# Ten equal token blocks of 464 and 456 columns in place of nine of 512

## The chip, the cores and the metric

The kernel runs on one core of one Trainium2 chip. The metric is the device time of one execution in microseconds. TensorE multiplies, VectorE and ScalarE do the elementwise work, the DMA engines move data between the chip's memory and the core's buffers; SP and ScalarE issue the DMAs.

## What is computed

An attention over packed tokens, then two feed-forward blocks; only the last one is touched by the change. 4608 tokens, all in float32:

```python
x = sm_attn(q, p_packed, p_packed)            # 4608 x 512, p_packed = sm_attn(p, k, v)
a = x @ w1; b = x @ w2                         # 512 -> 1024
x = (a * b @ w3) @ w_out                       # 1024 -> 512
h = x @ w_in                                   # 512 -> 2048
g = np.where(h >= 1, h, np.where(h <= -1, 0.0, (h + 1) ** 2 / 4))
out = g @ w_out2                               # 2048 -> 512
```

## The kernel before

Everything is kept transposed: features on the 128 partitions, tokens along the columns. A product in float32 accuracy is made of three passes over a high and a low part (`PASSES`), so each 128x128 block of weights meets each block of tokens in three matmuls.

The two last products, `x @ w_in` and `g @ w_out2`, are each done as a 2x2 block product with seven block products in place of eight (names A11, S1, S2, A12, S4, S3, A22). One of the two halvings is over the tokens, so tokens go in pairs of blocks. `PAIRS` (line 31) has the first token and the width N of each pair: four pairs of 2 x 512 columns and a short one of 2 x 256.

The first product is the loop over `steps` (line 1057): 8 steps per pair, 40 in all. A step multiplies the seven block products for one block of 128 of the hidden features, six matmuls of N columns each (line 863, 42 per step). ScalarE copies the results of A11, S1 and S2 out of PSUM (`copy`, line 936), VectorE adds the copies to A12, S4 and S3 (`add`, line 940), and ScalarE and VectorE apply the piecewise square (`upper`, `lower_begin`, `lower_relu`, `lower_middle`: lines 871, 874, 877) and the subtractions that the second product's block form needs (`upper_end`, line 904; `lower_end`, line 929). A22 of a step comes one step later, behind S2 of the next step; for the last step it follows at once (line 1112). Results go to the chip's memory, `gd`, from SP's queue (line 888). Two weight tiles per step, `ws`, are loaded in each step.

While a pair is multiplied, the operands of the next pair are made from `x2f` (`x2_tasks`: eleven tasks, seven of them a ScalarE copy, line 730, and a VectorE subtraction, line 731, four a VectorE subtraction alone, line 715). `MID`, `LAST` and `LAST_SHORT` say after which products of which step how many tasks are issued. In the short pair `lower_end` stands ahead of the second addition, the `x2s` tiles hold two operands each, and two steps share an `L` tile.

In the last pair `first_sides` loads what the second product needs first. The second product is the loop over `seq` (line 1160): per pair seven products of four tiles, each tile 12 matmuls of N columns (line 1169). Each tile's operand is loaded from `gd` (`g_load`, line 1007, at most six tiles ahead), for A22 first combined of two loads (line 1016), and split into a high and a low part by ScalarE (line 1024) and VectorE (line 1025). During the first pair five more weight operands are loaded (`w2_load`, line 974) and partly split (lines 982, 983). Results leave by `evacuate` (copies at line 1142, additions at line 1146) and ScalarE's queue (line 1152).

There is no scheduler: each engine works through its instructions in the order in which they are written.

Of the kernel before, what the change touches and what calls it, by code (L numbers as in the profile page):

```python
# [9 lines left out]
F32R = mybir.dt.float32r  # L10
# [12 lines left out]
P = 128  # L23
# [4 lines left out]
CHS = [min(CH, S - i * CH) for i in range(NCH)]  # L28
XD = NT

PAIRS = [(0, 512), (1024, 512), (2048, 512), (3072, 512), (4096, 256)]

A11, S1, S2, A12, S4, S3, A22 = range(7)
STREAM = (S4, A22)
# [25 lines left out]
def fused_kernel(ctx: ExitStack, tc, qT, kT, vv, pb, w1, w2, w3T, wo, win, wout, out):  # L60
# [9 lines left out]
    w2d = [dram.tile([P, 8, 256] if i in PLAIN else [P, 8, 2, 256], F32, name=f"w2{i}") for i in range(7)]  # L70
    gd = [dram.tile([P, 6, 8, n], F32, name=f"g{i}") for i, (_, n) in enumerate(PAIRS)]

# [304 lines left out]
    late = {}  # L377
# [132 lines left out]
    kept = []  # L510
# [189 lines left out]
    x2_t = {}  # L700

    def x2_load(t):
        t0, N = PAIRS[t]
        f = late["f"].tile([P, 4, 1024], F32, name="f", tag="f", bufs=1)
        nc.sync.dma_start(out=f[:, :, :2 * N], in_=x2d[0][:, :, t0:t0 + 2 * N])
        for r in range(2):
            for c in range(2):
                x2f[10 * r + c + 11] = f[:, 2 * r:2 * r + 2, c * N:(c + 1) * N]

    def x2_tasks(t):  # L710

        N = PAIRS[t][1]

        def combine(dst, a, b):
            return lambda: nc.vector.tensor_tensor(out=x2f[dst], in0=x2f[a], in1=x2f[b], op=ALU.subtract)

        room = []

        def parts(q, src):
            def f():  # L720
                if not room:
                    x = late["b1"].tile([P, 2, 2, 512], F32R, name="x2s", tag="x2s", bufs=9)
                    if N == 512:
                        room.append(x)
                    else:
                        x = x.rearrange("p a b (c n) -> p (a b c n)", n=N).rearrange(
                            "p (o a b n) -> p o a b n", o=2, a=2, b=2)
                        room.extend([x[:, 0], x[:, 1]])
                x = x2_t[t, q] = room.pop(0)
                nc.scalar.activation(out=x[:, 0, :, :N], in_=x2f[src], func=AF.Copy)  # L730
                nc.vector.tensor_tensor(
                    out=x[:, 1, :, :N], in0=x2f[src], in1=x[:, 0, :, :N].bitcast(F32), op=ALU.subtract)
            return f
        return [
            parts(A11, 11), combine(11, 12, 11), combine(12, 22, 12), parts(S1, 11), combine(11, 22, 11),
            parts(S2, 11), parts(A12, 21), parts(S4, 22), parts(S3, 12), combine(11, 21, 11), parts(A22, 11),
        ]

    for b in range(1, B):
# [4 lines left out]
        else:  # L744
            spread = {}
            late["f"] = tc.alloc_tile_pool(name="fp", bufs=1, side="left", reuse_waits="tile")
            b1 = late["b1"] = tc.alloc_tile_pool(name="b1", bufs=1, side="left", reuse_waits="tile")
# [43 lines left out]
    def buf(tag):  # L791
        if tag in first:
            return first.pop(tag)
        shape, bufs = KINDS[tag]
        return hp.tile(shape, F32, name=tag, tag=tag, bufs=bufs)
# [9 lines left out]
    def ws_tile(x):  # L805
        return wp.tile([P, 2, 2, P], F32R, name=f"ws{x}", tag=f"ws{x}", bufs=2)

    def ws_load(s, x, eng):
        if s < 8 * len(PAIRS):
            t = ws_t[s, x] = first.pop(f"ws{x}", None) or ws_tile(x)  # L810
            eng.dma_start(out=t.bitcast(F32), in_=wst[s % 8 // 4][:, s % 4, x])
# [37 lines left out]
    def product(s, q):  # L849
        t, i = divmod(s, 8)  # L850
        N = PAIRS[t][1]
        b = BANK[q]
        if q in (A11, S1, A12):
            bank[s, b] = psb(b)
        n, c0 = divmod(i, 4)
        j = 0
        for k in range(2):
            for v, m in PASSES:
                if q in STREAM:
                    w = ws_t[s, STREAM.index(q)][:, k, v, :]  # L860
                else:
                    w = wi_t[q, n][:, k, v, c0 * P:(c0 + 1) * P]
                nc.tensor.matmul(  # L863
                    bank[s, b][:, :N], w, x2_t[t, q][:, m, k, :N],
                    start=(j == 0 and q in (A11, S1, A12)), stop=(j == 5), skip_group_check=True,
                )
                j += 1
# [11 lines left out]
    kept = {}  # L879
# [6 lines left out]
    def store(s, a, n, x):  # L886
        t, i = divmod(s, 8)
        stores.append(lambda: nc.sync.dma_start(out=gd[t][:, a:a + n, i], in_=x))

    def upper(s):  # L890

        N = PAIRS[s // 8][1]
        h = kept[s, 0]
        r = buf("r")[:, :, :N]
        relu(r, h[:, :2, :N])
        square(r)
        for c in range(2):
            smaller(h[:, c, :N], h[:, c, :N], r[:, c])
        store(s, G11, 1, h[:, 0:1, :N])

    def upper_end(s):
        N = PAIRS[s // 8][1]
        h = kept[s, 0]
        nc.vector.tensor_tensor(out=h[:, 2, :N], in0=h[:, 1, :N], in1=h[:, 0, :N], op=ALU.subtract)
        store(s, GT1, 1, h[:, 2:3, :N])

    def lower_begin(s):
        N = PAIRS[s // 8][1]
        r = kept[s, "r"] = buf("r")[:, :, :N]
        relu(r[:, 1], kept[s, 1][:, 1, :N])  # L910

    def lower_relu(s):
        N = PAIRS[s // 8][1]
        relu(kept[s, "r"][:, 0], bank[s, "x"][:, :N])

    def lower_middle(s):

        N = PAIRS[s // 8][1]
        h, r, ps = kept[s, 1], kept[s, "r"], bank.pop((s, "x"))[:, :N]
        square(r)  # L920
        smaller(h[:, 0, :N], ps, r[:, 0])
        smaller(h[:, 1, :N], h[:, 1, :N], r[:, 1])
        store(s, G21, 2, h[:, :2, :N])
        flush_stores()

    def lower_end(s):
        N = PAIRS[s // 8][1]
        h = kept.pop((s, 1))
        nc.vector.tensor_tensor(
            out=h[:, 2:4, :N], in0=h[:, 1:2, :N].to_broadcast([P, 2, N]), in1=kept.pop((s, 0))[:, 1:3, :N],  # L930
            op=ALU.subtract)
        store(s, GT3, 2, h[:, 2:4, :N])

    def copy(tag, ps, N):
        c = buf(tag)[:, :N]
        nc.scalar.activation(out=c, in_=ps[:, :N], func=AF.Copy)  # L936
        return c

    def add(out, ps, c, N):
        nc.vector.tensor_tensor(out=out, in0=ps[:, :N], in1=c, op=ALU.add)  # L940
# [4 lines left out]
    def tasks(n):  # L945
        for _ in range(n):
            if todo:
                todo.pop(0)()
# [80 lines left out]

    MID = {7: 1, 0: 1}  # L1030
    LAST = {2: 2, 3: 1, 4: 1, 5: 1, 7: 2, 0: 1}
    LAST_SHORT = {2: 2, 3: 2, 4: 1, 5: 1, 6: 1, 7: 2, 0: 1}


    def first_sides(s):
# [21 lines left out]
    for s in range(steps):  # L1057
        t, i = divmod(s, 8)
        N = PAIRS[t][1]
        if i == 1 and t + 1 < len(PAIRS):  # L1060
            if t:
                x2_load(t + 1)
            todo = x2_tasks(t + 1)
        if i == 0:
            tasks(1)
        product(s, A11)
        m1 = copy("m1", bank[s, "x"], N)
        if s:
            upper(s - 1)
            if i:  # L1070
                upper_end(s - 1)
            lower_begin(s - 1)
        product(s, S1)
        m5 = copy("m5", bank[s, "z"], N)
        product(s, S2)
        u2 = copy("u2", bank[s, "x"], N)
        if s:
            product(s - 1, A22)
            lower_relu(s - 1)
            lower_middle(s - 1)  # L1080
        product(s, A12)
        kept[s, 0] = buf("U")
        add(kept[s, 0][:, 0, :N], bank.pop((s, "y")), m1, N)
        short = t + 1 == len(PAIRS) and i
        if short:
            lower_end(s - 1)
        to_short = t + (i > 0) + 1 == len(PAIRS)
        tasks(0 if to_short else MID.get(i, 0))
        if t + 1 < len(PAIRS):
            kept[s, 1] = buf("L")  # L1090
        else:
            if s % 2 == 0:
                both = buf("L")
            kept[s, 1] = both[:, :, s % 2 * N:(s % 2 + 1) * N]
        product(s, S4)
        ws_load(s + 2, 0, nc.scalar)
        add(kept[s, 0][:, 1, :N], bank.pop((s, "z")), u2, N)
        product(s, S3)
        add(kept[s, 1][:, 1, :N], bank[s, "x"], m5, N)
        if i == 7 and not short:  # L1100
            lower_end(s - 1)
        tasks((LAST_SHORT if to_short else LAST).get(i, 0))
        if s and i < 7 and not short:
            if i == 0:
                upper_end(s - 1)
            lower_end(s - 1)
        ws_load(s + 1, 1, nc.sync)
        flush_stores()
        for w in {0: (A11, S1), 1: (S2, A12, S3)}.get(s, ()):
            wi_load(w, 1)  # L1110
        first_sides(s)
# [48 lines left out]
    for x, (t, q, j) in enumerate(seq):  # L1160
        N = PAIRS[t][1]
        b = BANK[q]
# [82 lines left out]
```

## Time and profile before

| | us |
|---|---|
| median of 3 runs (1269.65 to 1274.02) | 1270.3 |
| the profiled execution | 1274.56 |
| its span | 1272.8 |
| TensorE busy with matmuls | 1253.5 |
| VectorE busy | 842.1 |
| ScalarE busy | 695.0 |
| first of the two last products begins | 558.4 |
| second of them begins | 918.9 |

Busy time of a matmul contains its drain, which overlaps with the next one; so the distance between the starts of two groups tells what a matmul costs in a row, and idle time in front of a group is shown with the instruction that ended it.

### The profile page before, as it was taken

To read this page: it belongs to the slowest core of one execution; us is meant where nothing else is said; L and a number is where in the kernel's file an instruction comes from. 1 tells how busy PE (TensorE), PEld (TensorE's weight loads), DVE (VectorE), ACT (ScalarE), POOL (GpSimd) and SP (SyncE) were. 2 spreads that over 40 slices of the span, in tenths; PEclk is the share of its full clock that TensorE was granted. 3 is DMA by queue.
4 is the path that set the end of the run, shared out by engine and by line. 5 is a ranking of instruction groups with operands and counts; after the bars stand their busy time and mean duration, and the time that the engine had idled before them with its cause. 6 is when DMAs were issued, how large, how long until landed. Compare 5 with 4: busy or idle time off the path is not lost.

```text
span 1272.8 us, 21501 instructions
## 1 busy us (share of the span) xinstructions
PE 1253.5 (98%) x8344; PEld 1058.3 (83%) x8344; DVE 842.1 (66%) x1356; ACT 695.0 (55%) x1184; POOL 0.7 (0%) x6
## 2 busy tenths in 40 slices
PE   8999999999999999999999999999999999999998
PEld 4468899999989999988888888888888788888888
DVE  3675787857777766707788877878757546464555
ACT  5774546454645553516676767766755443425343
POOL 0000000000000000000000000000000000000000
PEclk9999999999999999999999999999999999999999
DMA  8872566645656533278676586767999868577675
GB/s 317 312 272 84 180 217 209 231 141 212 210 191 232 178 126 135 100 283 310 226 254 247 198 298 221 245 226 255 354 380 330 316 205 293 195 254 272 215 231 183
DMA packets 125302, 297.11 MB, mean 233 GB/s; under 512 B 11024, under 2 KB 47888, under 8 KB 120720
## 3 DMA queue, kind: packets, MB, share of 16 engines
q1 hardware_dynamic: 91888, 241.73, 54.4%
q10 hardware_dynamic: 33312, 54.01, 12.3%
q8 instruction: 65, 1.06, 0.3%
q14 instruction: 37, 0.30, 0.1%
HBM read 195.04 MB, written 100.66 MB: 232 GB/s over the span
## 4 chain that ended last, share of the span: by engine, by line
PE 83%; DMA 7%; ACT 6%; DVE 3%; issue 1%; SPq 0%; ACTq 0%; DVEq 0%
PE psk L417 16%; PE x L1169 15%; PE psk L393 14%; PE x L863 12%; PE z L1169 7%; PE z L863 6%; PE y L1169 4%; PE y L863 3%; PE psk L186 3%; PE psk L521 2%; ACT r L871 1%; DMA raw<-w3T 1%; PE psm L186 1%; ACT x2s L730 1%; ACT r L874 1%
## 5 line engine op out<-in xcount | busy, mean ns | idle before, releaser
L393 PE MATMUL psk<-at,m 128*128 128x288 f32 x1536 | 218.6, 298 | 0.3 <-DVE tb L405 0.3
L393 PEld LDWEIGHTS psk<-at,m 128*128 128x128 f32 x1536 | 205.9, 188 | 13.4 <-issue 7.0
L417 PEld LDWEIGHTS psk<-g,w 128*128 128x128 f32 x1536 | 204.8, 188 | 12.9 <-ACT m L107 8.4
L417 PE MATMUL psk<-g,w 128*128 128x288 f32 x1536 | 210.3, 296 | 0.0
L863 PE MATMUL x<-x2s,wi 128*128 128x512 f32 (+1 forms) x720 | 163.3, 371 | 1.4 <-ACT m L936 1.0
L863 PEld LDWEIGHTS x<-x2s,wi 128*128 128x128 f32 x720 | 126.1, 188 | 27.2 <-ACT m L936 3.7
L1025 DVE TENSOR_TENSOR op<-raw,op 128x1024 fp32r<-128x1024 f32 (+1 forms) x94 | 101.7, 1113 | 70.3 <-ACT op L1024 70.2
L1024 ACT ACTIVATE op<-raw 128x1024 fp32r<-128x1024 f32 (+1 forms) x94 | 87.3, 965 | 70.8 <-DVE raw L1016 31.9
L1169 PE MATMUL x<-op,w 128*128 128x512 f32 (+1 forms) x480 | 102.2, 372 | 2.0 <-DVE op L1025 1.7
L1169 PE MATMUL x<-op,hwi 128*128 128x512 f32 (+1 forms) x480 | 100.4, 368 | 0.0
L1169 PEld LDWEIGHTS x<-op,w 128*128 128x128 f32 x480 | 84.8, 191 | 18.6 <-DVE op L1025 2.6
L1169 PEld LDWEIGHTS x<-op,hwi 128*128 128x128 f32 x480 | 83.1, 188 | 15.8
L405 DVE TENSOR_TENSOR tb<-psk,ta 128x288 f32<-128x288 f32 x128 | 57.9, 454 | 49.8 <-ACT ta L403 29.7
L874 ACT ACTIVATE r<-r 128x1024 f32<-128x1024 f32 (+1 forms) x80 | 78.0, 975 | 2.5
L1025 DVE TENSOR_TENSOR op<-r,op 128x1024 fp32r<-128x1024 f32 (+1 forms) x46 | 50.2, 1117 | 39.1 <-ACT op L1024 39.1
L877 DVE SCALAR_TENSOR_TENSOR U<-U,r 128x512 f32<-128x512 f32 (+1 forms) x80 | 47.5, 635 | 38.4 <-ACT r L874 38.4
L403 ACT ACTIVATE ta<-psk 128x288 f32<-128x288 f32 x128 | 51.5, 404 | 30.5 <-PE psk L393 27.9
L936 ACT ACTIVATE m<-x 128x512 f32<-128x512 f32 (+1 forms) x40 | 22.1, 553 | 84.1 <-PE x L863 66.7
L1024 ACT ACTIVATE op<-r 128x1024 fp32r<-128x1024 f32 (+1 forms) x46 | 43.2, 969 | 41.0 <-DVE r L1016 16.1
L128 ACT ACTIVATE cvt<-raw 128x512 f32<-128x512 f32 (+1 forms) x74 | 49.0, 662 | 28.7 <-DMA raw<-w3T 9.4
L108 DVE TENSOR_TENSOR m<-psk,m 128x512 fp32r<-128x512 f32 x62 | 38.7, 684 | 39.1 <-ACT m L107 39.1
L107 ACT ACTIVATE g<-tb 128x288 fp32r<-128x288 f32 x128 | 56.3, 440 | 11.6 <-DVE tb L405 11.5
(115 smaller groups left out, 1851.7 us busy)
## 6 DMA issues: line engine op xcount, KB each, us to landing
raw<-g SPq DMA_DIRECT2D x86, 512.0 KB, 5.1
g<-L SPq DMA_DIRECT2D x64, 512.0 KB, 3.8
r<-g SPq DMA_DIRECT2D x42, 512.0 KB, 5.3
g<-U SPq DMA_DIRECT2D x64, 256.0 KB, 2.1
ws<-ws SPq DMA_DIRECT2D x42, 256.0 KB, 4.2
v<-vv SPq DMA_DIRECT2D x8, 1280.0 KB, 8.3
wi<-hl ACTq DMA_DIRECT2D x20, 512.0 KB, 3.6
wi<-wi SPq DMA_DIRECT2D x10, 1024.0 KB, 7.7
```

The costliest lines, as they stand in the source:

```text
L107: nc.scalar.activation(out=dst[:, 0], in_=src, func=AF.Copy)
L128: nc.scalar.activation(out=t, in_=words.bitcast(F32)[:, :, 1], func=AF.Prelu, scale=2.0 ** -112, alpha=2.0 ** 32)
L186: nc.tensor.matmul(ps[r][NP * q:NP * q + NP], stat[64 * r:64 * r + 64, NP * q:NP * q + NP], mov(q)[64 * r:64 * r + 64], start=True, stop=True,
L393: nc.tensor.matmul(ps[w][:, :HS], m_tile[b, w, n][:, s, G, c0 * P:(c0 + 1) * P], at_tile[b][:, G, v, hf * HS:(hf + 1) * HS], start=(k == 0 ...
L403: nc.scalar.activation(out=bs, in_=ps[1][:, :HS], func=AF.Copy)
L405: nc.vector.tensor_tensor(out=g, in0=ps[0][:, :HS], in1=bs, op=ALU.mult)
L417: nc.tensor.matmul(ps, w34[kt][:, s, mt * P:(mt + 1) * P], g_t[kt, hf][:, v, :], start=(kt == kts[0] and n == 0), stop=(kt == kts[-1] and ...
L863: nc.tensor.matmul(bank[s, b][:, :N], w, x2_t[t, q][:, m, k, :N], start=(j == 0 and q in (A11, S1, A12)), stop=(j == 5), skip_group_check= ...
L874: nc.scalar.activation(out=r, in_=r, func=AF.Square)
L1024: nc.scalar.activation(out=o[:, :, 0, :N], in_=a[0], func=AF.Copy)
L1025: nc.vector.tensor_tensor(out=o[:, :, 1, :N], in0=a[0], in1=o[:, :, 0, :N].bitcast(F32), op=ALU.subtract)
L1169: nc.tensor.matmul(bank[b][d][:, :N], w2_t[q][j // 2][:, 2 * (j % 2) + k, s, d * P:(d + 1) * P], op[x][:, k, v, :N], start=start and k == ...
```

## The change

`PAIRS` holds five pairs now, three of 2 x 464 and two of 2 x 456 columns; all that treated the short pair in its own way is gone. Every step has one order, that of the long pairs. The matmuls are as many as before. In the tiles, which keep their size, 464 or 456 of 512 columns are used; so a load of two rows of `gd` into one tile is no longer one run of 4096 bytes per partition, but two of 1856 or 1824.

```diff
-PAIRS = [(0, 512), (1024, 512), (2048, 512), (3072, 512), (4096, 256)]
+PAIRS = [(0, 464), (928, 464), (1856, 464), (2784, 456), (3696, 456)]
...
-        room = []
-
         def parts(q, src):
             def f():
-                if not room:
-                    x = late["b1"].tile([P, 2, 2, 512], F32R, name="x2s", tag="x2s", bufs=9)
-                    if N == 512:
-                        room.append(x)
-                    else:
-                        x = x.rearrange("p a b (c n) -> p (a b c n)", n=N).rearrange(
-                            "p (o a b n) -> p o a b n", o=2, a=2, b=2)
-                        room.extend([x[:, 0], x[:, 1]])
-                x = x2_t[t, q] = room.pop(0)
+                x = x2_t[t, q] = late["b1"].tile([P, 2, 2, 512], F32R, name="x2s", tag="x2s", bufs=9)
...
-    LAST_SHORT = {2: 2, 3: 2, 4: 1, 5: 1, 6: 1, 7: 2, 0: 1}
...
-        short = t + 1 == len(PAIRS) and i
-        if short:
-            lower_end(s - 1)
-        to_short = t + (i > 0) + 1 == len(PAIRS)
-        tasks(0 if to_short else MID.get(i, 0))
-        if t + 1 < len(PAIRS):
-            kept[s, 1] = buf("L")
-        else:
-            if s % 2 == 0:
-                both = buf("L")
-            kept[s, 1] = both[:, :, s % 2 * N:(s % 2 + 1) * N]
+        tasks(MID.get(i, 0))
+        kept[s, 1] = buf("L")
         product(s, S4)
...
-        if i == 7 and not short:
+        if i == 7:
             lower_end(s - 1)
-        tasks((LAST_SHORT if to_short else LAST).get(i, 0))
-        if s and i < 7 and not short:
+        tasks(LAST.get(i, 0))
+        if s and i < 7:
```

On VectorE, one step of the last pair stood so before (L929 is `lower_end`, L940 an addition, `m` and `u` the copies, L877 the piecewise square of the next round):

```order
L940 TENSOR_TENSOR U<-y,m_9868 128x256
L929 TENSOR_TENSOR L<-L,U 128x2x256
L940 TENSOR_TENSOR U<-z,u_9893 128x256
L940 TENSOR_TENSOR L<-x,m_9885 128x256
L877 SCALAR_TENSOR_TENSOR U<-U,r 128x256 x2
```

and now (the same lines are L930, L919 and L867):

```order
L930 TENSOR_TENSOR U<-y,m_9871 128x456
L930 TENSOR_TENSOR U<-z,u_9896 128x456
L930 TENSOR_TENSOR L<-x,m_9888 128x456
L919 TENSOR_TENSOR L<-L,U 128x2x456
L867 SCALAR_TENSOR_TENSOR U<-U,r 128x456 x2
```

`lower_end` moved behind the two additions. On VectorE, the change from the fourth pair's last step to the last pair's first stood so before (L731 and L715 are the tasks that make the next pair's operands):

```order
L940 TENSOR_TENSOR U<-y,m_9705 128x512
L940 TENSOR_TENSOR U<-z,u_9730 128x512
L940 TENSOR_TENSOR L<-x,m_9722 128x512
L929 TENSOR_TENSOR L<-L,U 128x1024
L731 TENSOR_TENSOR x2s<-f,x2s 128x512 x2
L715 TENSOR_TENSOR f<-f 128x2x256
L877 SCALAR_TENSOR_TENSOR U<-U,r 128x512 x2
L877 SCALAR_TENSOR_TENSOR L<-x,r 128x512
L877 SCALAR_TENSOR_TENSOR L<-L,r 128x512
L940 TENSOR_TENSOR U<-y,m_9788 128x256
```

and now:

```order
L930 TENSOR_TENSOR U<-y,m_9701 128x456
L721 TENSOR_TENSOR x2s<-f,x2s 128x2x456
L930 TENSOR_TENSOR U<-z,u_9726 128x456
L930 TENSOR_TENSOR L<-x,m_9718 128x456
L919 TENSOR_TENSOR L<-L,U 128x2x456
L721 TENSOR_TENSOR x2s<-f,x2s 128x2x456 x3
L867 SCALAR_TENSOR_TENSOR U<-U,r 128x456 x2
L867 SCALAR_TENSOR_TENSOR L<-x,r 128x456
L867 SCALAR_TENSOR_TENSOR L<-L,r 128x456
L930 TENSOR_TENSOR U<-y,m_9790 128x456
L715 TENSOR_TENSOR f<-f 128x2x456
```

One splitting task moved ahead of the second addition, and one combining task went behind the next step's first addition.

## Rows read from the trace of the kernel before

**Rows 1.** Stretches: us, busy and count of PE, PEld, DVE, ACT, POOL; clock, DMA share, GB/s.

```profile
640.00:717.00 77.00, 76.88 (x336) 62.65 (x335) 61.62 (x84) 53.84 (x71) 0.00 (x0) 1.00 0.69 244
...
871.00:918.90 47.90, 44.37 (x342) 41.95 (x340) 35.36 (x81) 33.81 (x69) 0.00 (x0) 0.99 0.96 328
918.90:931.00 12.10, 12.10 (x49) 9.90 (x49) 6.97 (x10) 5.93 (x8) 0.00 (x0) 0.89 1.01 350
...
986.00:997.00 11.00, 9.33 (x40) 6.86 (x38) 6.29 (x8) 3.54 (x4) 0.00 (x0) 1.00 1.00 371
997.00:1074.00 77.00, 77.00 (x338) 63.44 (x339) 42.67 (x40) 32.71 (x37) 0.00 (x0) 1.00 0.72 249
...
1227.00:1257.00 30.00, 30.00 (x253) 29.60 (x252) 13.77 (x24) 14.81 (x29) 0.00 (x0) 1.00 0.72 227
```

**Rows 2.** The chain of waits, TensorE alone: start us, us, what.

```profile
734.39 2.75 PE x L863 x12
...
882.15 1.41 PE x L863 x12
...
1043.52 10.99 PE x L1169 x48
...
1065.39 21.76 PE x L1169 x96
...
1240.63 5.44 PE x L1169 x48
```

**Rows 3.** Timeline of TensorE at 288 columns: start us, us, line, operation, count.

```profile
501.71 3.43 PE L417 MATMUL psk<-g,w 128*128 128x288 f32 x24
```

**Rows 4.** Timeline of TensorE, from the first to the second pair.

```profile
646.84 2.91 PE L863 MATMUL x<-x2s,wi 128*128 128x512 f32 x12
649.58 1.54 PE L863 MATMUL z<-x2s,wi 128*128 128x512 f32 x6
651.25 1.65 PE L863 MATMUL x<-x2s,wi 128*128 128x512 f32 x6
```

**Rows 5.** Timeline of TensorE, first step; in brackets idle us and who ended it.

```profile
565.41 1.89 PE L863 MATMUL y<-x2s,wi 128*128 128x512 f32 x6 [2.66 <-DMA wi<-wi]
```

**Rows 6.** Timeline of TensorE in the short pair and at its end.

```profile
877.21 0.86 PE L863 MATMUL z<-x2s,wi 128*128 128x256 f32 x6
879.05 0.97 PE L863 MATMUL x<-x2s,wi 128*128 128x256 f32 x6 [0.98 <-ACT m L936]
...
893.11 1.57 PE L863 MATMUL x<-x2s,wi 128*128 128x256 f32 x12
...
898.55 1.57 PE L863 MATMUL x<-x2s,wi 128*128 128x256 f32 x12
...
914.90 0.87 PE L863 MATMUL x<-x2s,wi 128*128 128x256 f32 x6
917.78 1.28 PE L863 MATMUL x<-x2s,ws 128*128 128x256 f32 x6 [2.02 <-DVE L L940]
...
931.09 4.23 PE L1169 MATMUL z<-op,hwi 128*128 128x512 f32 x17
```

**Rows 7.** Timeline of all engines, S3 and its addition in a long pair.

```profile
782.29 2.91 PE L863 MATMUL x<-x2s,wi 128*128 128x512 f32 x12
...
784.04 0.68 DVE L940 TENSOR_TENSOR L<-x,m 128x512 f32<-128x512 f32 x1
```

**Rows 8.** Timeline of all engines at the end of the kernel.

```profile
1256.79 5.92 PE L1169 MATMUL z<-op,w 128*128 128x256 f32 x48
...
1267.66 1.57 PE L1169 MATMUL x<-op,w 128*128 128x256 f32 x11 [0.34 <-DVE op L1025]
...
1269.27 0.38 ACT L1142 ACTIVATE U<-x 128x256 f32<-128x256 f32 x1 [0.33 <-PE x L1169]
1269.68 0.38 ACTq L1152 DMA_DIRECT2D out<-U  x1
```

**Rows 9.** DMA issues: tiles, queue, count, KB each, us to landing.

```profile
out<-U ACTq DMA_DIRECT2D x8, 512.0 KB, 4.6
```

## The prediction

> **What bounds the kernel now.** I read the table of stretches first [rows 1]. In a pair of 512 columns of the first of the two products TensorE works 76.88 of 77.00 us, in one of the second product 77.00 of 77.00, while VectorE works 61.62 of 77.00 us and less. So TensorE sets the time, and the reader should look for two things alone: what one matmul costs at each width, and where TensorE stands idle. The same table shows three places where it does: the short pair (871 to 918.9 us, 44.37 of 47.90 us busy), the stretch 986 to 997 (9.33 of 11.00 us) and, outside it, the end. It also shows that the DMA engines are full in the three stretches that lie between 871 and 997 us (shares 0.96 to 1.01) and at 0.69 to 0.72 in the others.
>
> Then the chain of waits gives the price of a matmul where nothing interrupts it [rows 2]: 2.75/12 = 229.2 ns at 512 columns in the first product, 1.41/12 = 117.5 at 256. In the second product the groups of 48 take 10.99 us (five of seven) and 21.76/2 = 10.88 us (the other two), and 5.44 at 256 columns, so 228.3 on average and 113.3. Both products have 8 x 7 x 6 = 336 matmuls per pair (the second: 7 x 4 x 12). The content of both is 1344 x 0.2292 + 336 x 0.1175 + 4 x (5 x 10.99 + 2 x 10.88) + 7 x 5.44 = 692.4 us. The two stages last from 558.4 us to about 1269.2 us, so some 18 us are waiting and slow starts. Only these 18 us, and the price of a matmul at the new widths, can change.
>
> **The price at 464 and 456 columns.** The number of matmuls stays 3360 and so does the sum of their columns (per loop position 4 x 512 + 256 = 3 x 464 + 2 x 456). No row shows either width. By a straight line between 256 and 512 columns the prices are 208.3 and 204.8 ns in the first product, 206.7 and 203.1 in the second, together 692.4 us: no change. The only other width in long runs is 288 [rows 3]: 24 matmuls in 3.43 us, of which the last one's drain is about 0.17 (twelve matmuls show 2.91 us [rows 4] where the next group begins 2.74 after them), so 135.8 ns, where the line has 131.5. A line from 288 to 512 gives 209.2 and 205.9, 208.5 and 205.2 ns, in all 4.9 us more. The run of 24 belongs to another loop and may hold a restart, so I take half: **+2.4 us**. Lower end: every matmul at the cheapest rate seen, 226.7 ns for 512 columns, gives 685.6 us, -6.8. Upper end: the 4.3 ns by which 288 lies over the line, on all 3360, is +14.4.
>
> **The waits, one by one.**
> Start of the first product: TensorE waits 2.66 us for a weight load [rows 5]. The 18 matmuls ahead of it get shorter by 18 x 0.021 = 0.4 us, the load does not come earlier: **+0.4** (0 to 0.4).
> Changes of pair: the second step of each pair begins S2 0.30 us late (1.67 instead of 1.37 us [rows 4]), three times, since the copy of A11's result queues on ScalarE behind the last task that prepares the next pair; on entering the short pair 1.84 - 0.71 = 1.13 us. After the change four equal ones. The five products of TensorE that cover the chain shorten by 30 x 0.021 = 0.6 us. If the chain shrinks in proportion a wait is 0.27 us, if not at all 0.9; its parts have fixed and column-wise shares, so 0.45: 1.8 instead of 2.0, **-0.2** (-0.9 to +1.7).
> Inside the short pair a step takes 5.44 us (893.11 to 898.55 [rows 6]), its 42 matmuls 4.94. Seven such steps lose 3.5 us, because the operations of ScalarE and VectorE follow one another at half the width while TensorE's cover is halved. At 512 columns a step shows nothing of the kind, and 464 and 456 are near that: **-3.5** (-3.5 to 0). In the new order lower_end stands behind both additions, as in the long pairs; its store on SP's queue goes out two additions later, and ahead of the same loads as before. The tasks of the pair before it return to the long pairs' places, which they hide in already.
> Last step: A22 follows S3 at once and has to wait for VectorE's addition. It begins 2.88 us after S3 began, whose matmuls need 0.71: 2.17 us idle. Then 1.61 us more are lost, since from 917.78 to 931.09 there are 13.31 us for 0.71 + 10.99 of matmuls [rows 6], and the granted clock in that stretch is 0.89 [rows 1], part of it at 1.2 GHz after the idle stretch. In a long pair without tasks S3 begins at 782.29 and ends 1.37 later, and the addition ends at 784.72, 1.06 us behind it [rows 7], because it has less queued in front. So 1.1 us idle replaces 2.17, and shorter idle stretches than 1 us show no fall of the clock (0.98 us ahead of 879.05 [rows 6]; the clock of 871 to 918.9 is 0.99): -1.1 - 1.6 = **-2.7** (-2.7 to 0).
> First pair of the second product: DMA share 1.00 and 1.01 at 350 to 371 GB/s, and TensorE idles 1.67 us towards its end [rows 1]. The loads of the second weights (five of the six operands still to come, and half of another) keep their size while the pair has 48/512 less time: by the order of SP's queue that is 1 + 3 + 1 + 2 = 7 MB, at some 357 GB/s 20 us, of which 9.4% is 1.9 us. The g loads shrink with the pair, but each partition's 4096 bytes become two pieces of 1856. Pieces of 1024 bytes move 227 GB/s at share 0.72, whole ones 249 at the same share [rows 1]; in between that is about 4% of 15 MB, 1.7 us. Against both stands that the queue is no longer full when the stage begins: the last pair has its stores and loads spread over 70 us, not 48. **+2** (0 to +5).
> End of the second product: 1256.79 to 1267.66 holds 85 matmuls, 85 x 0.1133 = 9.6 us in 10.9 [rows 8]: the last operand needs a subtraction and a split per tile, and VectorE's pair of them is as long as TensorE's 12 matmuls. At 512 columns the same place runs 96 matmuls in 21.76 us without a gap [rows 2]: **-1.2** (-1.2 to 0).
> Behind the last matmul: the last copy (0.38 us) grows by some 0.2, and the last store from 256 to 456 KB. It takes 3.1 us to the end of the span now [rows 8]; a 512 KB one takes 4.6 [rows 9], in between +1.2, though those share the engines with other work: together **+1.0** (0.2 to 1.5).
> Sum of the waits: 0.4 - 0.2 - 3.5 - 2.7 + 2.0 - 1.2 + 1.0 = -4.2. With the matmuls' +2.4: **-1.8 us**. The profiled execution took 1274.56 us (span 1272.8), 4.3 over the median of 1270.3; on that median the forecast is 1268.5.
>
> **Rivals.**
> Faster: the streams run at the cheapest rate, as two of seven operands do now at 512 columns. Then -6.8 - 4.2: 1259.3. For it: widths that are no power of two need not be dearer at all, and 113.3 ns at 256 is the same rate. Against: three quarters of today's long matmuls pay 229, and 288 pays more.
> Slower: each matmul of an in-between width pays the 4.3 ns that 288 shows: +14.4 - 4.2, 1280.5. It decides from 3.2 ns a matmul on (10.6 us, which with -4.2 is +6.4). For it: the 288 row. Against: 464 is 48 columns from 512, and the excess may be a restart.
> The loads: the g blocks' rows of 1856 bytes begin at multiples of 64 bytes. If a read that begins off a 256-byte line also moves what lies below it, on average 96 of 1856 bytes, 5% of 15 MB at 357 GB/s is 2.2 us more in the full stretch: 1270.7. The Trainium skill, "DMA: Bandwidth & Descriptors", section "How a descriptor splits into AXI transactions", says this of descriptors that do not begin 256-byte aligned; no row here has such reads to show it, so the sum leaves it out.
> Nothing gained at the last step: the idle time and the slow clock stay, +2.7: 1271.2.
>
> **How the numbers follow.** Forecast 0.45, the two that stay near it (loads, last step) 0.13, faster 0.25, slower 0.17. A measurement of this kernel can tell about 0.5%, 6.4 us, from no change. So faster 0.25 (under 1263.9), same 0.58, slower 0.17 (over 1276.7). The forecast's own range is 1264 to 1274; to leave out no more than 2 in 10, half of either outer case is taken in: 1260 to 1280.
>
> **What would show it.** In the new profile: groups of 48 matmuls at 464 columns in 9.9 to 10.0 us (9.86 or less for the faster rival, 10.1 and more for the slower); a step of the last pair at 42 matmuls' time, near 8.6 us; A22 of the last step about 1.1 us behind S3, and no stretch of low clock there; idle time of 3 to 4 us in the first pair of the second product with the DMA share at 1; no gap among the last 100 matmuls. The prediction is wrong at its root if TensorE waits in every step, at any place, since 0.1 us a step is already 4 us.

## The result: 0.62% slower, and the profile after

The changed kernel takes 1280.03 us (median of 4 runs, 1277.94 to 1282.03), the kernel before, measured beside it, 1270.24 us (median of 4): ratio 1.0062, 95% interval 1.0045 to 1.0079. That is slower, by a little more than the 0.5% that the prediction named as what a measurement can tell; the forecast was no change that can be told. (Before there were eight blocks of 512 columns and two of 256, which hold as many columns as the nine of 512 in the title.) The profiled execution took 1282.03 us, its span is 1280.2 us, 7.4 us over the span of before.

Where the 7.4 us come from is read in the same three views. First the table of stretches (columns as in [rows 1]):

```profile
870.00:918.00 48.00, 47.08 (x227) 42.30 (x226) 32.24 (x52) 29.95 (x44) 0.00 (x0) 1.00 0.88 292
918.00:930.00 12.00, 11.10 (x50) 8.64 (x48) 7.74 (x10) 5.00 (x7) 0.00 (x0) 1.00 0.97 321
930.00:938.00 8.00, 5.24 (x17) 4.34 (x18) 4.41 (x4) 4.58 (x6) 0.00 (x0) 0.79 1.04 398
938.00:988.00 50.00, 50.00 (x240) 44.77 (x239) 36.42 (x44) 28.31 (x39) 0.00 (x0) 1.00 1.02 357
988.00:1058.00 70.00, 70.00 (x336) 62.62 (x335) 37.49 (x39) 29.66 (x36) 0.00 (x0) 1.00 0.74 250
```

The reader is to see that the waits of the short pair are gone (47.08 of 48.00 us busy, where [rows 1] had 44.37 of 47.90), that the wait late in the first pair of the second product is gone too (50.00 of 50.00, then 70.00 of 70.00), and that a new hole stands at the start of that product: 5.24 of 8.00 us, at a granted clock of 0.79, with the DMA engines full.

Second, the price of a matmul, from the chain of waits (start us, us, what), as in [rows 2]:

```profile
605.01 2.52 PE x L853 x12
...
862.27 2.49 PE x L853 x12
...
1045.50 10.08 PE z L1149 x48
1055.58 20.16 PE x L1149 x96
...
1246.01 9.96 PE x L1149 x48
1255.97 10.01 PE z L1149 x48
1265.98 10.04 PE x L1149 x48
```

At 464 columns 2.52/12 = 10.08/48 = 210.0 ns in both products; at 456 columns 207.5 ns, with three of seven operands in the second product at 208.5 to 209. The content of the two products is now 1008 x 0.210 + 672 x 0.2075 = 351.1 us and 3 x 70.56 + 2 x 69.90 = 351.5 us (a pair of 464 columns is 7 groups of 10.08; one of 456 is four of 9.96, one of 10.01 and two in 20.05), 702.6 in all. Before it was 692.4, by the prediction's sum (its parts are looked at again below). **The same columns in the same number of matmuls cost 10.2 us more.**

Third, the waits. From the first matmul of the first product (557.41) to the end of the last one of the second (1265.98 + 10.04 = 1276.02) there are 718.6 us, of which 16.0 are not content; before, 558.4 to 1269.2, 18.4. So the waits shrank by 2.4 us. The first matmul came 1.0 us earlier, and behind the last one there are 4.2 us to the end of the span, 0.6 more than before. 10.2 - 2.4 - 1.0 + 0.6 = 7.4.

The timeline of TensorE shows the waits that are left: at the start of the first product, a new one 40 us later, one of 0.31 us at a change of pair (642.76 to 644.33, 1.57 us for six matmuls of 1.26), the last step, and the start of the second product.

```profile
557.41 1.42 PE L853 MATMUL x<-x2s,wi 128*128 128x464 f32 x6
...
563.75 2.16 PE L853 MATMUL y<-x2s,wi 128*128 128x464 f32 x6 [2.39 <-DMA wi<-wi]
...
600.96 1.53 PE L853 MATMUL x<-x2s,ws 128*128 128x464 f32 x6 [1.36 <-DVE L L930]
...
642.76 1.42 PE L853 MATMUL z<-x2s,wi 128*128 128x464 f32 x6
644.33 0.90 PE L853 MATMUL x<-x2s,wi 128*128 128x464 f32 x3
...
901.95 1.41 PE L853 MATMUL x<-x2s,ws 128*128 128x456 f32 x6
...
910.67 0.57 PE L853 MATMUL x<-x2s,ws 128*128 128x456 f32 x2
...
914.40 1.41 PE L853 MATMUL x<-x2s,wi 128*128 128x456 f32 x6
916.72 1.51 PE L853 MATMUL x<-x2s,ws 128*128 128x456 f32 x6 [0.92 <-DVE L L930]
...
918.77 5.57 PE L1149 MATMUL x<-op,w 128*128 128x464 f32 x24 [0.32 <-DVE op L1015]
924.83 5.09 PE L1149 MATMUL x<-op,w 128*128 128x464 f32 x23 [0.48 <-DVE op L1015]
932.08 0.48 PE L1149 MATMUL z<-op,hwi 128*128 128x464 f32 x1 [2.15 <-ACT op L1014]
```

Who is late at 932.08 is seen in the timeline of all engines: the loads of `r` (the operand of the next block product) are issued on SP's queue at 924.23, behind the last stores of the first product, and ScalarE, which splits `r`, waits 6.88 us for them.

```profile
922.62 1.51 SPq L878 DMA_DIRECT2D g<-L  x2
924.23 1.23 SPq L997 DMA_DIRECT2D r<-g  x2
931.05 0.98 ACT L1014 ACTIVATE op<-r 128x928 fp32r<-128x928 f32 x1 [6.88 <-DMA r<-g]
```

At the end, where [rows 8] had a gap, there is none; the last store follows the last copy.

```profile
1265.82 10.19 PE L1149 MATMUL x<-op,w 128*128 128x456 f32 x48
1276.05 0.55 ACT L1122 ACTIVATE U<-x 128x456 f32<-128x456 f32 x1 [0.70 <-PE x L1149]
1276.62 0.38 ACTq L1132 DMA_DIRECT2D out<-U  x1
```

### The profile page after: what moved, and what is told of

Read it like the earlier page. It is cut to its first block, busy times and chain, and to the rows that moved or that the text cites. A ratio compares the mean times of both kernels' runs of the same rounds, so it can differ in the third digit from the quotient of the medians.

```text
span 1280.2 us, 21504 instructions
## 1 busy us (share of the span) xinstructions
PE 1258.9 (98%) x8344; PEld 1102.4 (86%) x8344; DVE 842.1 (66%) x1356; ACT 693.8 (54%) x1184; POOL 0.7 (0%) x6
## 4 chain that ended last, share of the span: by engine, by line
PE 86%; DMA 8%; ACT 3%; DVE 2%; issue 1%; SPq 0%; DVEq 0%; ACTq 0%
PE psk L393 16%; PE psk L417 16%; PE x L1149 15%; PE x L853 12%; PE z L1149 8%; PE z L853 6%; PE y L1149 4%; PE y L853 3%; PE psk L186 3%; DMA raw<-w3T 2%; DMA wi<-wi 2%; DMA g<-L 1%; DMA raw<-w 1%; PE psm L186 1%; DMA raw<-wo 1%; ACT cvt L128 1%
## 5 line engine op out<-in xcount | busy, mean ns | idle before, releaser
L853 PE MATMUL x<-x2s,wi 128*128 128x464 f32 (+1 forms) x720 | 164.5, 373 | 0.6 <-ACT m L926 0.3
L1015 DVE TENSOR_TENSOR op<-raw,op 128x928 fp32r<-128x928 f32 (+1 forms) x94 | 101.8, 1115 | 71.5 <-ACT op L1014 71.4
L1014 ACT ACTIVATE op<-raw 128x928 fp32r<-128x928 f32 (+1 forms) x94 | 87.3, 966 | 73.9 <-DVE raw L1006 32.1
L1149 PE MATMUL x<-op,w 128*128 128x464 f32 (+1 forms) x480 | 102.2, 372 | 0.8 <-DVE op L1015 0.8
L1149 PE MATMUL x<-op,hwi 128*128 128x464 f32 (+1 forms) x480 | 102.0, 371 | 0.0
L1149 PEld LDWEIGHTS x<-op,hwi 128*128 128x128 f32 x480 | 90.1, 188 | 10.2
L864 ACT ACTIVATE r<-r 128x928 f32<-128x928 f32 (+1 forms) x80 | 78.0, 975 | 2.5
L1015 DVE TENSOR_TENSOR op<-r,op 128x928 fp32r<-128x928 f32 (+1 forms) x46 | 50.1, 1115 | 42.5 <-ACT op L1014 42.4
L867 DVE SCALAR_TENSOR_TENSOR U<-U,r 128x464 f32<-128x464 f32 (+1 forms) x80 | 47.4, 634 | 35.8 <-ACT r L864 35.7
L1014 ACT ACTIVATE op<-r 128x928 fp32r<-128x928 f32 (+1 forms) x46 | 43.1, 966 | 38.8 <-DVE r L1006 14.5
L521 PE MATMUL psk<-wo,w3f 128*128 128x512 f32 x128 | 58.1, 601 | 5.0 <-DVE w3f L141 4.3
```

The lines of the kernel that those rows point to most:

```text
L521: nc.tensor.matmul(acc[4 * hf + m], w3f[hf, j][:, m * P:(m + 1) * P], wof[j], start=(j == 0), stop=(j == 7))
L853: nc.tensor.matmul(bank[s, b][:, :N], w, x2_t[t, q][:, m, k, :N], start=(j == 0 and q in (A11, S1, A12)), stop=(j == 5), skip_group_check= ...
L864: nc.scalar.activation(out=r, in_=r, func=AF.Square)
L1014: nc.scalar.activation(out=o[:, :, 0, :N], in_=a[0], func=AF.Copy)
L1015: nc.vector.tensor_tensor(out=o[:, :, 1, :N], in0=a[0], in1=o[:, :, 0, :N].bitcast(F32), op=ALU.subtract)
L1149: nc.tensor.matmul(bank[b][d][:, :N], w2_t[q][j // 2][:, 2 * (j % 2) + k, s, d * P:(d + 1) * P], op[x][:, k, v, :N], start=start and k == ...
```

## Experiments: what a matmul costs at each width

The theory after the result: the width itself sets the price, and in-between widths are dear. The rivals: the other engines' and the DMAs' work on the same buffers makes them dear, or the place of the columns in memory does.

**p_width.** Only matmuls, in the order of the first product's, 96 in a row for each of 29 widths (512 a second time ahead of them), with nothing else at work.

```diff
+    def run(N):
+        for g in range(GROUPS):
+            b = banks[g % 7]
...
+            for k in range(2):
+                for v, m in PASSES:
+                    mov = flat[:, (2 * m + k) * N:(2 * m + k + 1) * N] if PACKED else x[:, m, k, :N]
+                    nc.tensor.matmul(b[:, :N], wi[:, k, v, g % 4 * P:(g % 4 + 1) * P], mov,
...
```

> Only matmuls, nothing else runs beside them: 96 in a row at each of 30 widths from 256 to 512 columns, in groups of six over the same three passes, weights and moving operand laid out as in the first product (no part of the reference is computed). Theory 1, the width sets the price: 210 ns at 464, 207.5 at 456 and 229 at 512 come back here with no other engine at work, and every width but a few lies 2 to 6 ns above 226.7/512 = 0.4428 ns a column, in steps and not on a line. Rival, other traffic sets it: here 464 costs 205.4 and 456 201.9, the cheapest rate of the kernel before. Second rival, a fixed extra per matmul: all widths on one line, with 208.3 at 464.

The table of stretches (us, busy and count of PE and PEld, ...), each stretch the time from the first of 96 matmuls to the first of the next width (the counts include neighbours that overlap): 256, 288, 464, 456, 496 and 512 columns.

```profile
34.94:46.45 11.51, 11.51 (x97) 11.51 (x96) 0.00 (x0) 0.00 (x0) 1.00 0.00 0
58.48:71.13 12.65, 12.65 (x99) 12.65 (x98) 0.00 (x0) 0.00 (x0) 1.00 0.01 1
234.77:254.93 20.16, 20.16 (x98) 17.99 (x97) 0.00 (x0) 0.00 (x0) 1.00 0.00 1
440.41:460.44 20.03, 20.03 (x98) 18.00 (x96) 0.00 (x0) 0.00 (x0) 1.00 0.00 1
275.73:296.85 21.12, 21.12 (x98) 18.02 (x97) 0.00 (x0) 0.00 (x0) 1.00 0.00 1
296.85:318.61 21.76, 21.76 (x98) 18.02 (x97) 0.00 (x0) 0.00 (x0) 1.00 0.00 0
```

Divided by 96: 119.9, 131.8, 210.0, 208.6, 220.0, 226.7 ns (and 146.6 at 320, 173.3 at 384). So 464 and 456 columns cost with nothing else at work what they cost in the kernel: the other engines' traffic is not the cause. A straight line from 256 to 512 gives 206.7 at 464 and 203.3 at 456; the matmuls lie 3.3 and 5.3 ns above it, while 288 lies 1.5 ns below its 133.3. Per column 512 is the cheapest of these (0.4428 ns; 464 takes 0.4526, 456 takes 0.4575, 256 takes 0.4683). At five of these eight widths the price is a multiple of 6.67 ns (18, 22, 26, 33 and 34 of them at 256, 320, 384, 496 and 512: one for 16 columns and two more); 464 and 456 lie half a step and more above that pattern.

**p_packed.** The same with the rows of the moving tile side by side (row `i` begins at column `i x N` in place of `i x 512`).

```diff
-PACKED = False
+PACKED = True
```

> As the run of widths alone, but the four rows of the moving operand stand side by side, each N columns long, and not each at the start of its own 2048 bytes (no part of the reference is computed). If the extra price comes from where a row begins or from columns left unused at a row's end, prices change here, by 2 ns or more at 464 and 456; if the width alone sets it, each width costs the same as in the run before within 0.5 ns.

464 columns cost 209.3 ns, 456 cost 205.6, 448 cost 206.5 (202.8 in p_width), 496 223.4 and 512 226.8. Moving where the rows begin shifts a price by up to 4 ns, up or down. So width is the larger part, but place has one too.

**p_place.** The same matmuls with the moving columns shifted by 0 to 384 columns against a fixed beginning.

```diff
+                    mov = far[:, (2 * m + k) * 512 + o:(2 * m + k) * 512 + o + N]
```

> Only matmuls (no part of the reference is computed): 96 in a row at each of six widths (512, 496, 464, 456, 320, 256) and each of ten starts of the moving operand, shifted by 0 to 384 columns. Theory 1a, the width alone sets the price: one price per width at all ten starts, within 0.5 ns, 210 at 464. Rival 1b, the price is a matter of where weights and tokens lie to one another: at some starts 464 costs 205 to 207 and at others 210 or more, and 512 shows both 226.7 and 229, which the kernel before shows for its two kinds of weight tiles.

The table of stretches, 96 matmuls each: 512 columns shifted by 0, 16 and 32; 456 and 256 by 16.

```profile
36.32:58.08 21.76, 21.76 (x97) 18.02 (x96) 0.00 (x0) 0.00 (x0) 1.00 0.00 0
80.49:102.47 21.98, 21.98 (x97) 18.03 (x96) 0.00 (x0) 0.00 (x0) 1.00 0.00 1
102.47:124.77 22.30, 22.30 (x97) 18.09 (x96) 0.00 (x0) 0.00 (x0) 1.00 0.00 1
...
711.27:731.18 19.91, 19.91 (x97) 18.02 (x96) 0.00 (x0) 0.00 (x0) 1.00 0.00 0
...
1034.95:1046.26 11.31, 11.31 (x99) 11.31 (x97) 0.00 (x0) 0.00 (x0) 1.00 0.00 0
```

512 columns take 226.7, 229.0 and 232.3 ns. At shifts of 0 and 16 columns 464 take 209.0 and 209.9, 456 take 208.8 and 207.4, 256 take 120.0 and 117.8. At shifts of 64 columns (256 bytes) and its multiples 512 takes 226.7 each time. Neither expectation holds whole: the price isn't one at all ten starts, but no start brings 464 columns below 208.8. The shift of 16 columns, 64 bytes, gives the kernel's own prices (229.2, 210.0, 207.5, 117.5), and 64 bytes is what lies, modulo 256, between the addresses that the program gives to its moving tiles (`x2s`, `op`: remainder 160) and to most of its weight tiles (`wi`, `ws`, `hwi`: 96). The weights in `w`, three of the seven operands of the second product, have the moving tiles' remainder, and there 512 columns cost 226.7 ns already before (21.76/96 in [rows 2]). So before the change the place made most of the long matmuls 2.3 ns dearer and the short ones of the first product 2.3 ns cheaper. The 113.3 ns of [rows 2] at 256 columns came at no start of p_place.

**a_place.** That can be tried in the kernel: a small tile that is allocated early is made longer, and all later moving tiles move up by 192 bytes, to the weights' remainder.

```diff
-    half = tmp.tile([P, 1], F32, name="half")
+    half = tmp.tile([P, 56], F32, name="half")[:, :1]
```

> The changed kernel with the one edit that moves its moving tiles by 192 bytes. Theory (price by width and place): measured alone, 464 columns cost 208.9 at equal remainders and 209.9 at 64 bytes apart, 456 columns 208.7 and 207.4; so the sum moves by less than 2 us and the median stays within 1276 to 1281, ratio to before 1.004 to 1.008. The place is thus not what the new widths suffer from; the width is. Rival (the place is what makes the widths dear): content falls towards 692 us, median about 1270.

1279.12 us, ratio 1.0056 (1.0039 to 1.0073): as the changed kernel. At 464 and 456 columns the place is worth nothing in sum that these runs can tell; what the new widths suffer from is the width.

**b_place.** The same edit on the kernel before.

> The kernel before with the one edit that moves its moving tiles by 192 bytes, so that they and the weight tiles begin at the same remainder of 256 bytes. Theory: 512 columns fall from 229.0 ns to 226.7 (2304 of the 2688 long matmuls pay 229), 256 columns rise from 117.6 to about 120 in the first product and from 113 to at most 120 in the second; content 690 in place of 692.4 us, so 2 to 4 us faster than before, ratio 0.997 to 0.999, if the waits stay. Rival: no change, ratio 1.000.

1269.46 us, ratio 0.9984 (0.9973 to 0.9995). Its chain of waits has the groups of 12 and of 48 at 512 columns at 226.7 ns (2.72/12, 10.88/48), and those of 256 at 120.0 (5.76/48) where [rows 2] has 113.3:

```profile
572.69 2.72 PE x L863 x12
...
949.69 10.88 PE y L1169 x48
...
1228.74 5.76 PE z L1169 x48
```

At these places the price inside the kernel is the one measured alone.

## Experiments: other widths, and the code without the widths

**a_512.** The changed kernel's code with the widths of before.

```diff
-PAIRS = [(0, 464), (928, 464), (1856, 464), (2784, 456), (3696, 456)]
+PAIRS = [(0, 512), (1024, 512), (2048, 512), (3072, 512), (4096, 256)]
```

> The changed kernel's code, with the widths of before (four pairs of 512 columns and one of 256): the code for the short pair alone is undone. Theory (the widths cost the time, by their price): the time is that of the kernel before within 4 us, 1267 to 1275, since matmuls cost 229 and 118 again. Rival (what was cut for the short pair is what costs): 1277 and more, with TensorE idle inside the short pair for more than the 3.5 us of before, as VectorE has lower_end and the fourth pair's tasks at the long pairs' places.

1276.62 us, ratio 1.0031 (1.0014 to 1.0047). The time lies between the two expectations. The matmuls cost what they did (2.75 us for 12, 10.88 and 10.99 for 48), so the loss of some 4 us lies in waits: without its own order the short pair waits longer at its first change and at its last step than [rows 6] shows (0.98 and 2.02 us idle there).

```profile
880.09 0.97 PE L853 MATMUL x<-x2s,wi 128*128 128x256 f32 x6 [2.04 <-ACT m L926]
...
920.39 1.65 PE L853 MATMUL x<-x2s,ws 128*128 128x256 f32 x6 [2.44 <-DVE L L930]
```

In the two profiled executions the first product, from its first matmul to the last A22, takes 361.25 us for 359.34, 1.9 us more; the rest of the 4 us no trace here places. So by the middle values the change has two halves: the simpler code costs 0.31%, and the equal widths about another 0.31% on top of it, which is +10.2 us of price against some 6 us of waits that they spare. The second half is a difference of two ratios, and no run gives its interval.

**a_384.** Widths that are cheaper by p_width: three pairs of 512 and two of 384.

```diff
+PAIRS = [(0, 512), (1024, 512), (2048, 512), (3072, 384), (3840, 384)]
```

> The changed kernel's code with pairs of 512, 512, 512, 384, 384 columns. Theory 1 (the price of a width is what made the change slower): 512 costs 229, and 384, if it is as good as 512 by column (171 to 172 ns), brings the matmuls back to about 693 us, 9 less than with 464 and 456; with the waits of the changed kernel 1269 to 1272 us. Rival (the waits made it slower): 1277 to 1281, like the changed kernel.

1278.12 us, ratio 1.0043 (1.0023 to 1.0063). 384 columns cost 173.3 ns as alone, which makes the content 3 x (77.0 + 76.6) + 1344 x 0.1733 = 694 us: the price came back. But the waits grew: from the first to the end of the last matmul there are 713.3 us, 19.3 more than the content, where the changed kernel has 16.0. In the timeline of TensorE, from the third to the fourth pair:

```profile
803.95 1.31 PE L853 MATMUL x<-x2s,wi 128*128 128x384 f32 x6 [1.17 <-ACT m L926]
...
819.78 1.32 PE L853 MATMUL x<-x2s,wi 128*128 128x384 f32 x6 [0.89 <-ACT m L926]
822.48 1.31 PE L853 MATMUL x<-x2s,ws 128*128 128x384 f32 x6 [1.38 <-DVE L L930]
```

The first step of 384 columns still has work of the 512-column step behind it on ScalarE and VectorE, and TensorE waits 1.17 us for it at 803.95. Two steps later something else holds it up: VectorE's additions wait for stores of `g` to free their buffers.

```profile
818.58 0.56 DVE L930 TENSOR_TENSOR U<-y,m 128x384 f32<-128x384 f32 x1 [2.23 <-DMA g<-U]
...
821.87 0.56 DVE L930 TENSOR_TENSOR L<-x,m 128x384 f32<-128x384 f32 x1 [2.26 <-DMA g<-L]
```

My expectation, which took the changed kernel's waits over, missed both.

**a_496.** Four pairs of 496 and one of 320, both cheap per column by p_width.

```diff
+PAIRS = [(0, 496), (992, 496), (1984, 496), (2976, 496), (3968, 320)]
```

> The changed kernel's code with four pairs of 496 columns and one of 320. Alone, 496 costs 220.0 ns, almost the rate of 512 at its cheapest, and 320 146.6. Theory (the price of the widths makes the changed kernel slower): 3360 matmuls in 690 us and not 702.5, so 12 us less than the changed kernel, 1265 to 1270 us, about as fast as before or a little faster. Rival (the waits decide): 1276 and more.

1279.8 us, ratio 1.0063 (1.0039 to 1.0088): a miss. In its chain 12 matmuls of the first product take 2.72 us and 48 of the second 10.88 (10.72 with the weights in `w`), 226.7 ns, as much as 512 columns and not the 220.0 of p_width. p_place has the same 226.6 ns for 496 columns at a shift of 16 columns (and 220.0 or 223.3 at shifts of 0 and 64 columns), which led to

**a_496_place.** a_496 with the edit of a_place.

> The code of the changed kernel with four pairs of 2 x 496 columns and one of 2 x 320, as in a_496, and one more edit: a small tile that is allocated early is made 192 bytes longer per partition, so that the moving tiles (x2s, op) and the weight tiles (wi, hwi) begin at the same remainder of 256 bytes; before they were 64 bytes apart. Nothing else differs. Theory (the price goes by the width and by where the moving columns lie against the weights): 496 columns fall from 226.0 ns to 220.0 (or to 223.3, as the matmuls measured alone at larger shifts), 320 stays at 146.7, so the two products need 690 to 699 us in place of 706, and the median comes to 1264 to 1272 us. Rival (the price in the kernel comes from the other engines' and the DMAs' work on the buffers, and the place matters only where TensorE works alone): 226 ns as in a_496, median 1278 to 1281.

1274.52 us, ratio 1.0016 (1.0002 to 1.0031), against 1.0063 without the edit; the span of the profiled execution went from 1279.1 to 1271.1 us. Its chain of waits:

```profile
570.24 2.64 PE x L853 x12
...
650.17 2.68 PE x L853 x12
...
938.77 10.72 PE x L1149 x48
```

220.0 ns in the first pair, 223.3 from the second on. That the price goes by the place is confirmed in the kernel. The span shows more than that: the execution of a_496 had two stretches of low clock (0.91 from 555 to 575 us, 0.89 from 915 to 930), that of a_496_place none there. The median misses the 1264 to 1272 that I expected by 2.5 us: the price is mostly the higher of the two that I had named, and I had taken the waits of one execution of a_496, which may be why; no run shows it.

## Experiments: the wait at the start of the second product

**a_loads_first.** In the changed kernel the first loads of `r` go out ahead of the last step's stores.

```diff
     lower_begin(steps - 1)
+    g_load()
```

> The changed kernel with one edit: after the first product the next loads of the second product are issued ahead of the last step's stores. Theory 1 (SP's queue): the loads that TensorE waits for at 930 us leave at about 920 instead of 924, the idle time between 918 and 938 us falls from about 5 to 2 or less and the slow clock goes, 2 to 4 us in all. Rival (the DMA engines are full there): the loads land no earlier, the time stays within 1 us. The price of the matmuls stays 210 and 207.5 ns, so the kernel stays slower than before by 4 to 8 us.

1278.31 us, ratio 1.0047 (1.0031 to 1.0064), some 2 us less than the changed kernel by the middle values; the two intervals overlap. The loads are issued at 914.96 in place of 924.23, and the matmuls at 924.85 no longer wait for them, but the ones behind do, for the weights:

```profile
924.85 5.21 PE L1150 MATMUL z<-op,hwi 128*128 128x464 f32 x24
931.84 6.83 PE L1150 MATMUL z<-op,hwi 128*128 128x464 f32 x24 [1.78 <-DMA hwi<-w]
```

The low clock comes again (0.79 from 930 to 938 us). With the DMA engines full in this stretch (shares of 1.02 from 918 to 930 us and 1.05 from 930 to 938), another order moves the wait to another load.

**b_loads_first** and **b_place_loads_first.** The same edit on the kernel before, alone and with that of b_place.

> The kernel before with one edit: the next loads of the second product are issued ahead of the last step's stores. If the DMA engines' fullness sets the idle time in the first pair of the second product, as the run with the same edit on the changed kernel says (the wait for g loads went and one for a weight came in its place), the time stays within 1 us of before. If SP's order sets it, the 1.7 us of idle time at 986 to 997 us go and the time falls by 1.5 to 2.5.

> The kernel before with both edits: the moving tiles 192 bytes up (b_place), and the first loads of the second product issued ahead of the last step's stores (b_loads_first). If the two gains add: 1266 to 1269 us, ratio about 0.996. If the gain of the one is taken back by the other's waits: as b_loads_first alone, 0.998.

1270.68 us, ratio 0.9983 (0.9966 to 0.9999), and 1268.3 us, ratio 0.9980 (0.9964 to 0.9996). By the middle values each of the two edits gives about 0.2%, and together no more; that they add isn't shown. What the loads' order gives isn't shown by the trace either: in b_loads_first the time from the last A22 to the end is 354.3 us for 355.0 before, and from 986 to 997 us TensorE still idles 1.13 us of the 1.67.

## Why the prediction was wrong

The step that failed is **the price at 464 and 456 columns**. I drew a line between two widths, saw 288 lie 4.3 ns above it, and took half: +2.4 us. It measured +10.2. The term was mis-sized by 7.8 us. The rival that I called slower came closest, a surcharge on the new widths, but at a smaller size and not as 288 pays it: 10.2 us are 3.0 ns a matmul, just under the 3.2 from which I had said it decides; with the waits not falling by 4.2 it decided all the same.

Two things were wrong in the step. Its witness was: p_width has 288 columns at 131.8 ns, so the 135.8 read from [rows 3] did hold something of a restart or of another loop. The chain of the kernel before has longer runs that would have shown it, 132.3 ns a matmul:

```profile
293.45 15.87 PE psk L417 x120
```

With that witness the term would have come out near zero, so that half of it went the right way was luck. And the line was wrong: 512 is the cheapest width by column (0.4428 ns; 496 takes 0.4435, 464 takes 0.4526), so equal blocks leave the cheapest width; and the 256 columns of before were cheap by their place. The Trainium skill, "TensorE: Matmul & The Clock Gate", section "Back-to-back issue gap", gives N/2.4 + 2.5 ns as the gap of an isolated matmul of N columns at the full clock, which it sets apart from the spacing in a stream; by it the price is linear in the columns, and equal sums of columns would cost the same. The streams here are not linear: 226.7 ns at 512, where it has 215.8, and 3 to 5 ns over a line at 464 and 456.

The prediction's sum for before also counts its groups wrongly: in the second product four of seven operands take 10.99 us at 512 columns and three 10.88, not five and two, and at 256 columns the three with weights in `w` take 120.0 ns and not 113.3. The two errors nearly cancel, and the content comes to 692.5 us; but of the gap that it saw at the end of the second product 0.5 us was price.

The waits, forecast and measured:

| step of the prediction | forecast us | measured us |
|---|---|---|
| start of the first product | +0.4 | -0.3 (2.39 idle for 2.66) |
| changes of pair | -0.2 | -0.8 (4 x 0.31 for 2.0) |
| steps of the last pair | -3.5 | -3.5 (8.72 us from 901.95 to 910.67, 42 x 0.2075) |
| last step | -2.7 | -2.7 (S3 to A22 2.32 us for 1.25, and no low clock there) |
| first pair of the second product | +2 | +3.8 |
| end of the second product | -1.2 | -0.7 (no gap now; before, 85 x 0.120 = 10.2 of 10.9 us) |
| behind the last matmul | +1.0 | +0.6 |
| a wait at 600.96 | none | +1.4 |
| small pieces that I don't place | | +0.4 |
| sum | -4.2 | -1.8 |

The first pair's +3.8 is what is left of the second product: 6.4 us of waits now, 4.9 before, of which 1.6 stand under the last step and 0.7 under the end. The cause was as forecast, DMA engines that are full (1.02 and 1.04), but the place was not: I expected the wait late in the pair, where it was; it came at its start, behind the last stores, and with it came the low clock that I had counted as gone: it moved and was not saved. That the clock falls behind such an idle stretch is not certain either: b_place idles 2.00 us ahead of its last A22, where the kernel before idles 2.02, and keeps the full clock behind it (1.00 where [rows 1] has 0.89).

```profile
913.95 0.98 PE L863 MATMUL x<-x2s,ws 128*128 128x256 f32 x6 [2.00 <-DVE L L940]
...
918.90:931.00 12.10, 10.85 (x47) 8.45 (x46) 6.01 (x6) 6.04 (x7) 0.00 (x0) 1.00 1.02 376
```

The wait at 600.96 (VectorE's addition waits 2.57 us for a store of `g` to free its buffer) is not put to the widths: a_place has none there, a_loads_first has one of 0.64 us, and b_place_loads_first has one of 0.86 us at 670.53 with 512 columns.

That the first product began 1.0 us earlier was not forecast; nothing ahead of it is touched, and I don't explain it. In all: -1.8 forecast, +7.4 measured; the 9.2 between them are 7.8 of price and 2.4 of waits, less that 1.0. The medians differ by 2.4 us more than the two profiled executions, since that of before lies 4.3 us above its median, as the prediction said, and that of the changed kernel 2.0 above its own.

What stays open: why 464 and 456 columns lie above the steps of 6.67 ns; why at the same remainder 496 columns take 220.0 ns in one pair and 223.3 in the next, and 464 take 210.0 in p_width and 209.0 in p_place; and whether the loads pay for rows that begin off 256 bytes. In the second product the engines now move 250 GB/s at a share of 0.74, where [rows 1] has 249 at 0.72, but the pieces are smaller as well, and no run parts the two.

## What to carry to other kernels

Before blocks are made equal, measure a long run of matmuls at the very widths: where TensorE is the bound, 3 ns a matmul on 3360 matmuls outweighed the waits that the equal widths removed. A special order for a short block can be cheaper than no short block. And when a wait behind full DMA engines is removed, ask which load is late next: here it changed its place, twice.

## What the runs showed of the hardware

- The price of these matmuls is not linear in the columns: 226.7 ns at 512, 220.0 at 496, 210.0 at 464, 208.6 at 456, 173.3 at 384, 146.6 at 320, 119.9 at 256, with no other engine at work.
- It depends on where the moving columns lie against the weights, modulo 256 bytes: 512 columns 226.7, 229.0 and 232.3 ns at 0, 64 and 128 bytes, 256 columns 120.0 and 117.8 at 0 and 64. The remainder isn't all of it: 496 columns take 220.0 or 223.3 ns at the same one. Moving the moving tiles up by 192 bytes made the kernel before 0.16% faster (0.05 to 0.27%).
- TensorE's granted clock was 0.79 over the 8 us from 930 to 938 us in the changed kernel (0.50, 1.2 GHz, from 934 to 936), around and behind an idle stretch of 2.15 us, and 1.00 over the 12 us behind one of 0.92 us. The idle time alone doesn't decide it: the clock stayed at 1.00 behind 2.00 us in b_place, and over the 20 us from 555 to 575 us with an idle stretch of 2.82 us in a_place, where the changed kernel has 2.39 us and 0.91.
